# The last transform stage of a convolution, done once for all 640 channels

## The chip, the cores and the metric

The kernel runs on one core of one Trainium2 chip. The metric is device time in microseconds, the median of three runs. TensorE is called PE, its weight loads PEld, VectorE DVE, ScalarE ACT, GpSimd POOL, and SyncE, whose queue issues nearly all DMAs, SP.

## What is computed

Cut to what matters (S = 2048 rows, D = 640 channels, F = 1728):

```python
xn  = layernorm(x)                                   # x is A_q
ks  = sum_t  k_pad[:, t:t+S, :] * shift_k[:, 3 - t]  # four taps along the rows
kv  = ks * v
y   = irfft(rfft(kv, 4096) * rfft(ssm_k, 4096))[:, :S] + kv * ssm_D   # causal convolution per channel
A   = xn * y
B   = (sigmoid(xn @ w_gate) * (xn @ w_up)) @ w_down
out = x + A + B
```

## The kernel before

Two things share the core: the gated products B on PE, with their evictions, and the convolution A, whose four transform stages are small matmuls on PE with elementwise work between them.

**B.** The 2048 rows go in four blocks `tr` of 512. A block's normalized rows are transposed to `xnT`; then for each of 14 chunks `fc` of 128 hidden columns `rec_fc` (L761) makes a gate and an up product, five matmuls of 512 columns each (L773), and `rec_evac` makes `hT` from a sigmoid on ACT and a product on DVE (L727 to L740). `rec_down` (L780) then does the block's down product in pieces of seven matmuls of 320 columns (L789), added to `acc` by DVE (L800). `acc` holds x at first and the output in the end.

**A.** The 640 channels go in two halves, each in five groups of 64 channels; `idx` 0 to 9 counts the groups (`NI` = 10, `NSUB` = 5). A group's way:
- `rec_kv` (L451): ten DVE operations of 1024 elements for the taps (L469 to L474) and the product with v (L487) give `kvt`. The channel order inside a group is two runs of eight.
- `rec_st1` (L489): twice 32 matmuls on tiles of 32 rows (L507), of the filter (`ht`) and of `kvt`, evicted to `T`.
- `rec_st2` (L516): four times 32 matmuls (L527), evicted to `S`.
- `rec_prod` (L541): the complex product on DVE; from group 3 on a DMA swaps the halves of the partitions (`P<-S`, L547).
- `rec_st3` (L569): twice 8 matmuls of 128 columns (L579), evicted to `V`, a tile with all of one half: 64 × 2 × 80 columns.
- `rec_st4` (L595) per half, once its five groups are through: four units `u`, each in two parts of 64 matmuls on tiles of 32 × 32 (L611). A matmul has 80 columns, the channels of one quarter `g` of the half. Each unit reloads a piece of the normalized rows from memory (`xnd`, 512 pieces of 640 bytes), evicts twice 640 elements, and does two DVE operations of 1280 elements (L619, L620): times xn, plus `acc`.

`V` has one buffer, which first holds the early weights `wv` (gate and up, chunks 0 to 7, used by blocks 0 and 1), then the first half's V, then the second's. So the second half's first eviction to V waits for the first half's last stage. The reloads of the first half go to the two `xq` buffers (which hold normalized rows before), those of the second to the buffers of k and v. The PSUM tags are `c` (three slots of two banks) and `g` (two slots of one).

**Order.** Nothing is scheduled when it is built: every operation is recorded by `_Plan.op` (L152) with what it reads and writes, and `ORDER` (L80) lists in which order all 979 are issued; `ON_DVE` (L124) names those evictions that DVE does in ACT's place. `_Plan.emit` (L193) gives out buffers in that order. Each engine and the SP queue take their own operations in this order. In ORDER the first half's eight parts of L611 stand between stage 2 of group 6 and stage 3 of group 5, and the second half's between the last stage 3 and the down products of block 3. The last two row tiles' down products (`PRM["ML"]` = 14) also wait for the convolution's add (`cv`).

Of the kernel before, what the change touches and what calls it, by code (L numbers as in the profile page):

```python
# [18 lines left out]
S = 2048  # L19
# [16 lines left out]
NI = 2 * NSUB  # L36

# [5 lines left out]
def _dft_tables():  # L43
# [37 lines left out]
    1, 42, 5, 0, 6, 8, 7, 71, 72, 10, 12, 13, 11, 14, 73, 74, 75, 91, 86, 16, 87, 607, 76, 608, 4, 96, 77, 78, 97, 79,  # L81
    104, 88, 18, 60, 81, 82, 83, 625, 80, 92, 98, 643, 84, 85, 93, 99, 645, 89, 90, 63, 644, 94, 626, 43, 148, 100,
    62, 15, 66, 2, 149, 101, 102, 64, 150, 61, 68, 103, 621, 609, 623, 154, 611, 610, 622, 612, 624, 153, 67, 157,
    617, 619, 17, 65, 613, 158, 151, 59, 618, 615, 152, 650, 58, 620, 57, 651, 652, 56, 44, 29, 30, 627, 628, 629,
    630, 19, 31, 45, 32, 631, 633, 614, 616, 108, 20, 106, 632, 634, 639, 640, 641, 105, 39, 22, 155, 3, 642, 646, 24,
    599, 107, 156, 648, 647, 601, 600, 21, 26, 649, 635, 121, 109, 113, 602, 111, 603, 637, 27, 119, 604, 605, 112,
    606, 25, 636, 117, 638, 118, 663, 664, 666, 673, 110, 115, 116, 679, 122, 120, 123, 23, 125, 114, 674, 35, 37,
    677, 680, 133, 683, 681, 36, 653, 654, 682, 136, 684, 127, 661, 38, 162, 135, 657, 658, 134, 137, 662, 33, 675,
    665, 659, 660, 34, 130, 164, 47, 95, 676, 678, 667, 51, 128, 172, 163, 655, 656, 831, 165, 668, 671, 669, 49, 53,
    131, 739, 124, 166, 48, 50, 741, 28, 670, 832, 54, 126, 740, 167, 168, 833, 672, 742, 181, 183, 52, 689, 129, 691,  # L90
    721, 41, 171, 159, 723, 690, 692, 722, 132, 724, 298, 182, 160, 40, 694, 693, 696, 169, 161, 302, 730, 731, 732,
    733, 695, 697, 178, 716, 179, 180, 718, 743, 170, 173, 175, 195, 174, 300, 744, 745, 698, 717, 138, 197, 196, 176,
    177, 303, 201, 199, 700, 299, 185, 699, 198, 184, 187, 719, 720, 200, 685, 192, 301, 701, 186, 189, 702, 202, 686,
    687, 688, 188, 218, 203, 205, 707, 193, 204, 69, 46, 190, 194, 139, 709, 703, 708, 143, 217, 227, 207, 705, 141,
    55, 704, 710, 228, 229, 230, 706, 711, 191, 233, 140, 231, 725, 142, 305, 232, 812, 727, 712, 714, 213, 214, 726,
    206, 728, 713, 216, 219, 715, 734, 220, 772, 234, 221, 215, 209, 736, 210, 208, 222, 735, 737, 771, 224, 304, 746,
    70, 761, 226, 211, 729, 223, 212, 738, 749, 225, 252, 253, 762, 235, 764, 249, 251, 255, 263, 264, 236, 238, 254,
    750, 759, 752, 250, 265, 266, 269, 240, 267, 268, 747, 760, 237, 270, 256, 239, 748, 763, 288, 243, 290, 786, 751,
    257, 291, 244, 289, 788, 241, 260, 765, 242, 753, 271, 258, 261, 247, 766, 144, 245, 769, 272, 248, 262, 273, 754,
    757, 767, 285, 246, 287, 318, 407, 259, 768, 319, 275, 286, 294, 755, 296, 320, 410, 321, 274, 770, 324, 276, 322,  # L100
    277, 295, 787, 789, 325, 307, 278, 323, 292, 756, 758, 293, 834, 279, 280, 790, 281, 308, 836, 835, 837, 315, 326,
    309, 310, 282, 327, 782, 317, 297, 838, 811, 413, 283, 316, 306, 784, 312, 839, 311, 313, 783, 284, 785, 340, 341,
    354, 342, 355, 777, 840, 773, 329, 358, 867, 360, 146, 328, 356, 331, 409, 779, 775, 357, 359, 314, 330, 361, 774,
    778, 776, 780, 822, 351, 334, 335, 332, 791, 333, 362, 823, 343, 824, 363, 825, 344, 345, 412, 352, 145, 813, 353,
    815, 411, 336, 814, 147, 337, 338, 826, 346, 348, 404, 339, 816, 347, 383, 781, 408, 364, 366, 368, 369, 427, 817,
    828, 406, 365, 428, 827, 431, 376, 429, 405, 414, 433, 349, 829, 819, 430, 367, 818, 370, 371, 432, 792, 830, 820,
    372, 797, 434, 799, 373, 435, 866, 374, 793, 821, 350, 795, 436, 375, 806, 415, 418, 424, 425, 426, 794, 384, 796,
    416, 417, 463, 808, 419, 421, 464, 385, 386, 798, 387, 800, 388, 807, 377, 437, 389, 809, 465, 802, 466, 378, 810,
    801, 420, 804, 454, 439, 390, 379, 380, 803, 805, 449, 451, 438, 422, 450, 440, 467, 841, 842, 856, 843, 391, 443,
    468, 444, 469, 392, 423, 857, 846, 453, 859, 848, 393, 394, 460, 395, 470, 396, 397, 860, 9, 849, 861, 452, 455,  # L110
    886, 852, 864, 461, 457, 456, 441, 442, 881, 883, 462, 862, 398, 471, 399, 472, 401, 863, 400, 445, 926, 458, 446,
    490, 928, 489, 850, 447, 448, 459, 865, 851, 499, 500, 868, 870, 473, 505, 853, 488, 501, 502, 503, 854, 474, 476,
    475, 844, 506, 485, 479, 855, 487, 480, 845, 491, 477, 478, 847, 483, 504, 507, 858, 486, 484, 493, 481, 869, 508,
    482, 496, 492, 871, 498, 877, 497, 571, 494, 495, 578, 882, 521, 527, 509, 884, 510, 511, 512, 879, 522, 872, 878,
    887, 880, 523, 528, 533, 534, 513, 874, 529, 530, 531, 873, 875, 532, 514, 892, 515, 516, 524, 885, 893, 535, 894,
    536, 381, 907, 901, 585, 517, 876, 592, 525, 895, 519, 902, 526, 518, 549, 903, 402, 904, 896, 897, 905, 899, 888,
    906, 927, 537, 539, 898, 550, 890, 541, 538, 540, 542, 520, 553, 543, 554, 551, 555, 552, 929, 900, 545, 889, 544,
    556, 931, 891, 403, 557, 546, 558, 908, 910, 930, 932, 909, 547, 921, 911, 559, 923, 560, 917, 561, 919, 562, 922,
    918, 548, 924, 565, 566, 569, 563, 564, 570, 912, 920, 567, 913, 568, 572, 914, 915, 382, 573, 925, 933, 575, 934,
    938, 935, 916, 579, 580, 582, 574, 576, 581, 583, 584, 577, 963, 944, 965, 945, 586, 947, 939, 941, 587, 588, 589,  # L120
    936, 590, 591, 593, 594, 942, 596, 595, 970, 964, 597, 598, 937, 940, 943, 946, 973, 974, 967, 948, 950, 972, 949,
    966, 968, 952, 951, 969, 958, 953, 975, 954, 959, 962, 978, 955, 971, 960, 976, 956, 957, 961, 977
]
ON_DVE = [  # L124
    101, 103, 45, 133, 654, 136, 134, 34, 139, 426, 525, 895, 915, 575, 582, 589, 595
# [3 lines left out]
class _Op:  # L129
    __slots__ = ("engs", "alloc", "seq", "deps", "touch", "size", "on", "pri", "nb", "slack", "start", "end", "turn", "ni")  # L130


class _Plan:
# [18 lines left out]
    def op(self, engs, r=(), w=(), c=(), alloc=(), pri=0.0, size=0.0, nb=0.0, slack=0.0, ni=0):  # L152
        o = _Op()
        o.engs, o.pri, o.size, o.nb, o.slack, o.ni = engs, pri, size, nb, slack, ni
# [31 lines left out]
    def table(self):  # L186
        dve = set(ON_DVE)
        for i in ORDER:
            o = self.ops[i]
            o.on = next(iter(o.engs)) if len(o.engs) == 1 else "DVE" if i in dve else "ACT"  # L190
        return [self.ops[i] for i in ORDER]
# [27 lines left out]
def kernel(  # L219
# [23 lines left out]
    srow = A_shift_k.rearrange("(h g d) m -> g h (d m)", h=2, g=G)  # L243
    drow = A_ssm_D.rearrange("(h g d) -> g h d", h=2, g=G)
# [12 lines left out]
    ident = cst.tile([P, P], BF16, name="ident")  # L257
    acc = cst.tile([P, NQ, DM], BF16, name="acc")
    wd = cst.tile([P, NFC, DM], BF16, name="wd")
    Ft = cst.tile([P, 2 * K1 + 2 * P], U16, name="Ft")  # L260
    Mt = cst.tile([P, K1, 3 * K2], U16, name="Mt")
    At = cst.tile([P, 3, 2 * N2], U16, name="At")
    Bt = cst.tile([P, N2, 2, N1], U16, name="Bt")
    Fb = Ft.bitcast(F16)
# [7 lines left out]
    jk = cst.tile([P, DM], BF16, name="jk")  # L272
# [4 lines left out]

    SLOTS = {"w": 4, "xq": 2, "xnT": 1, "sig": 2, "bs": 1, "kt": 1, "vt": 1, "ht0": 1, "ht1": 1, "kvt": 2,
             "ta": 1, "tb": 1, "T": 2, "S": 2, "P2": 1, "V": 1, "c": 3, "g": 2}
    SHAPE = {  # L280
        "w": ([P, NC, 512], BF16), "xq": ([P, 4, DM], BF16), "xnT": ([P, NC, 512], BF16), "sig": ([P, 512], BF16),
        "bs": ([P, 12], F32), "kt": ([P, N2 + 3, HALF], BF16), "vt": ([P, N2, HALF], BF16),
        "ht0": ([P, 16, 2, N2], BF16), "ht1": ([P, 24, 2, N2], BF16), "kvt": ([P, 2, N2, JS], BF16),
        "ta": ([P, N2, 2, JS], BF16), "tb": ([P, N2, 2, JS], BF16), "T": ([P, 2 * K1, 2, JS, G], BF16), "S": ([P, 2, 2, JS, G * K1], BF16),
        "P2": ([P, 2, JS, G * K1], BF16), "V": ([P, N2, 2, HALF], BF16),
# [5 lines left out]
    def make(b, tag, i):  # L291
        shape, dt = SHAPE[tag]
        if b.startswith("pst"):
            shape, dt = [P, NC, P], BF16
        if b == "wv":
            shape, dt = [P, 4, NC, 512], BF16
        if b in ("xk", "xv"):
            shape, dt = [P, 2, 2, 4 * DM // 2], BF16
        pool = ps if tag in ("c", "g") else wk
        return pool.tile(shape, dt, name=f"{tag}{i}", tag=f"{tag}{i}")  # L300
# [149 lines left out]
    def by_j(t):  # L450
        return t.rearrange("p b n j -> p (b n j)").rearrange("p (j b n) -> p j b n", j=JS, b=2)  # L451
# [479 lines left out]
```

## Time and profile before

| what | value |
|---|---|
| median of 3 runs | 254.18 us (254.09, 254.18, 258.87) |
| span of the profiled execution (no other time of it is given) | 252.8 us |
| PE, DVE, ACT busy | 239.6, 202.2, 177.2 us |
| last stage, L611 on PE | 1024 matmuls, in two stretches: 152.6 to 169 and 223.7 to 236.4 us |
| first stage 1 of kv on PE | 67.98 us |
| last stage 3 on PE starts | 221.87 us |
| last matmul ends, last DVE operation ends | 247.5, 247.9 us |

The page of the profile gives busy times by engine and by slice; a group row gives line, engine, operation, output and inputs, shapes and count, then busy us and mean ns of one, then the engine's idle time just before them and what ended it. A matmul's own duration is mostly latency that overlaps the next one's, so its cost is read from the spacing, which the chain of work gives. Busy time on PE includes the end of the last matmul's latency.

### The profile page before, as it was taken

To read this page: it belongs to the slowest core of one execution; us is meant where nothing else is said; L and a number is where in the kernel's file an instruction comes from. 1 tells how busy PE (TensorE), PEld (TensorE's weight loads), DVE (VectorE), ACT (ScalarE), POOL (GpSimd) and SP (SyncE) were. 2 spreads that over 40 slices of the span, in tenths; PEclk is the share of its full clock that TensorE was granted. 3 is DMA by queue.
4 is the path that set the end of the run, shared out by engine and by line. 5 is a ranking of instruction groups with operands and counts; after the bars stand their busy time and mean duration, and the time that the engine had idled before them with its cause. 6 is when DMAs were issued, how large, how long until landed. Compare 5 with 4: busy or idle time off the path is not lost.

```text
span 252.8 us, 9452 instructions
## 1 busy us (share of the span) xinstructions
PE 239.6 (95%) x4211; PEld 145.6 (58%) x4245; DVE 202.2 (80%) x339; ACT 177.2 (70%) x260; POOL 0.7 (0%) x6
## 2 busy tenths in 40 slices
PE   7899999999999999999999999999999999999891
PEld 2754446764454557676554646677765554466571
DVE  4622635787999999999999999999999986878821
ACT  3723699686799997677998997867789886451100
POOL 1000000000000000000000000000000000000000
PEclk9999999999999999999999999999999999999998
DMA  6999999999993189699998995535617597001762
GB/s 173 336 299 241 278 214 159 174 132 211 226 144 104 65 245 233 141 148 127 175 195 227 244 226 141 91 75 167 130 29 175 135 275 191 3 3 31 158 174 62
DMA packets 90976, 41.44 MB, mean 164 GB/s; under 512 B 66736, under 2 KB 88056, under 8 KB 90616
## 3 DMA queue, kind: packets, MB, share of 16 engines
q1 hardware_dynamic: 90744, 40.52, 74.5%
q8 instruction: 33, 0.54, 1.0%
q10 hardware_dynamic: 192, 0.33, 0.4%
q14 instruction: 7, 0.06, 0.1%
HBM read 30.61 MB, written 5.24 MB: 142 GB/s over the span
## 4 chain that ended last, share of the span: by engine, by line
PE 66%; DVE 14%; DMA 7%; ACT 5%; issue 3%; ACTq 1%; SPq 0%; DVEq 0%
PE g L773 29%; PE g L789 20%; PE c L527 5%; PE c L611 3%; DMA P<-S 3%; PE c L579 3%; DMA w<-in_B_w_up_dram 2%; PE c L507 2%; ACT S L313 2%; DVE ta L474 2%; PE c L753 2%; DMA acc<-in_A_q_dram 1%; ACT sig L738 1%; DVE kvt L487 1%; DVE hT L740 1%
## 5 line engine op out<-in xcount | busy, mean ns | idle before, releaser
L773 PE MATMUL g<-xnT,w 128*128 128x512 bf16 x355 | 89.1, 379 | 2.4 <-DVE hT L740 0.5
L789 PE MATMUL g<-wd,hT 128*128 128x320 bf16 (+1 forms) x462 | 66.3, 295 | 0.2
L773 PEld LDWEIGHTS <-w 128*128 128x128 bf16 x380 | 35.0, 98 | 38.6 <-issue 1.3
L789 PEld LDWEIGHTS <-hT 128*128 128x128 bf16 x462 | 42.9, 98 | 16.8 <-issue 0.7
L313 ACT CAST S<-c 128x1024 bf16<-128x1024 f32 x40 | 40.0, 1031 | 2.8 <-PE c L527 2.3
L740 DVE TENSOR_TENSOR hT<-sig,g 128x512 bf16<-128x512 bf16 x32 | 21.9, 686 | 18.8 <-PE g L773 18.2
L773 PE MATMUL g<-xnT,V 128*128 128x512 bf16 x131 | 32.6, 379 | 0.6 <-DVE hT L740 0.2
L738 ACT ACTIVATE sig<-g 128x512 bf16<-128x512 f32 x32 | 19.5, 610 | 11.9 <-PE g L773 11.9
L313 ACT CAST V<-c 128x1024 bf16<-128x1024 f32 x20 | 20.4, 1026 | 4.8 <-PE c L579 3.7
L800 DVE TENSOR_TENSOR acc<-g,acc 128x320 bf16<-128x320 f32 (+1 forms) x33 | 15.6, 477 | 9.6 <-PE g L789 9.3
L527 PEld LDWEIGHTS <-Mt 64*128 64x128 f16 x1280 | 20.0, 95 | 5.5 <-issue 5.0
L316 ACT ACTIVATE T<-c 128x1024 bf16<-128x1024 f32 x20 | 20.2, 1032 | 3.7 <-PE c L507 3.6
L527 PE MATMUL c<-T,Mt 64*128 64x64 bf16 x1280 | 22.5, 190 | 0.2
L487 DVE TENSOR_TENSOR kvt<-ta,vt 128x1024 bf16<-128x1024 bf16 x10 | 21.5, 2146 | 0.1
L773 PEld LDWEIGHTS <-V 128*128 128x128 bf16 x140 | 13.0, 97 | 14.7 <-issue 0.8
L313 ACT CAST T<-c 128x1024 bf16<-128x1024 f32 x18 | 17.9, 1021 | 1.7 <-PE c L507 1.7
L732 ACT ACTIVATE sig<-g 128x512 bf16<-128x512 f32 x18 | 11.0, 610 | 7.6 <-PE g L773 5.9
L474 DVE TENSOR_TENSOR ta<-ta,tb 128x1024 bf16<-128x1024 bf16 x20 | 13.8, 689 | 0.4
L469 DVE TENSOR_TENSOR tb<-kt,sT 128x1024 bf16<-128x1024 bf16 x20 | 13.7, 683 | 0.1
L560 DVE TENSOR_TENSOR S<-S 128x1024 bf16<-128x1024 bf16 x20 | 13.5, 684 | 0.1
L579 PE MATMUL c<-At,S 128*128 128x128 f16 x160 | 12.8, 219 | 0.8 <-DVE S L566 0.7
L579 PEld LDWEIGHTS <-S 128*128 128x128 bf16 x160 | 10.8, 98 | 4.5 <-DVE S L566 2.1
(84 smaller groups left out, 243.6 us busy)
## 6 DMA issues: line engine op xcount, KB each, us to landing
w<-in_B_w_gate_dram SPq DMA_DIRECT2D x7, 640.0 KB, 6.4
w<-in_B_w_up_dram SPq DMA_DIRECT2D x7, 640.0 KB, 6.4
P<-S SPq DMA_DIRECT2D x14, 256.0 KB, 3.9
kt<-in_A_k_dram SPq DMA_DIRECT2D x8, 320.0 KB, 7.2
vt<-in_A_v_dram SPq DMA_DIRECT2D x8, 320.0 KB, 6.3
xnd<-xq SPq DMA_DIRECT2D x4, 640.0 KB, 5.1
ht<-in_A_ssm_k_dram SPq DMA_DIRECT2D x16, 96.0 KB, 4.6
wd<-in_B_w_down_dram SPq DMA_DIRECT2D x3, 480.0 KB, 10.2
```

The costliest lines, as they stand in the source:

```text
L313: fa = lambda: nc.scalar.copy(out=out_fn(), in_=in_fn())
L316: fa = lambda: nc.scalar.activation(out_fn(), in_fn(), ACT.Copy, scale=scale)
L469: dve(1024, 2, lambda: nc.vector.tensor_tensor(tl[c][:], sl(tl[kb], 3 - m), sh(m), ALU.mult) if c != o else nc.vector.tensor_tensor(tl[c]. ...
L474: dve(1024, 2, lambda: nc.vector.tensor_tensor(tl[a][:], tl[a][:], tl[c][:] if c != o else tl[c].rearrange("p b n j -> p n b j"), ALU.add) ...
L487: dve(1024, 1 if kt else 2, lambda: nc.vector.tensor_tensor(by_j(tl[o]) if kt else tl[o][:], tl[a].rearrange(form), sl(tl[vb], 0).rearrang ...
L527: nc.tensor.matmul(tl[c][:, b, 64 * kk:64 * kk + 64], lhsT=Mb[rows, k, 64 - 64 * r:192 - 64 * r], rhs=tl[T][rows, 2 * k + r].rearrange("p ...
L579: nc.tensor.matmul(o, lhsT=tl[S_][:, b, 0, j, :], rhs=Ab[:, 2 if zc else 0, :], start=True, stop=zc)
L738: act(512, lambda: nc.scalar.activation(tl[sg][:], pv(0), ACT.Sigmoid), r=[pk(0)], w=[(sg,)], alloc=[(sg, "sig")], pri=pri - 2000)
L740: dve(512, 1, lambda: nc.vector.tensor_tensor(hT[:, fc, :], tl[sg][:], pv(1), ALU.mult), r=[pk(1), (sg,)], w=[(hk, fc)], pri=pri - 2000)
L773: nc.tensor.matmul(tl[c][:], lhsT=w()[:, k, o:o + P], rhs=tl[X][:, k, :], start=(k == 0), stop=(k == NC - 1))
L789: nc.tensor.matmul(tl[pd[i]][:, 0:d1 - d0], lhsT=hT[:, fc, t4 * P:(t4 + 1) * P], rhs=wd[:, fc, d0:d1], start=(fc == 0), stop=(fc == NFC - 1))
L800: dve(d1 - d0, 1, lambda i=i, m=m, pd=pd, d0=d0, d1=d1: nc.vector.tensor_tensor(acc[:, m, d0:d1], tl[pd[i]][:, 0:d1 - d0], acc[:, m, d0:d1 ...
```

## The change

The last stage is done once, after all ten groups, for all 640 channels. `VV` is one tile of 21 chunks of 1024 columns; a group's V is two chunks, `Vc[:, idx]`. It shares memory with early buffers: chunks 0 to 9 with `wv`, chunks 10 to 15 with the two `xq` buffers, the scratch `jk`, the identity and the tables `FE`, chunks 16 to 20 with `ht`. `over` makes the first write of the second half's V wait for the users of `jk`, `ident` and `FE`, and groups 8 and 9 for those of `ht`. The quarter `g` now counts over all channels (`g * 160 + half * 80`), and a group's 16 channels of a quarter are one run, not two runs of eight; the filter is loaded with 16 DMAs in place of 32. A unit of `rec_st4` is 64 matmuls of 160 columns, whose moving operand is ten pieces of 16 columns; there are eight units. All reloads go to the buffers of k and v, in 256 pieces of 1280 bytes. The down products of the last two row tiles no longer wait for `cv`; the stores do. ORDER (956 operations) and ON_DVE are new.

```diff
-    ident = cst.tile([P, P], BF16, name="ident")
-    Ft = cst.tile([P, 2 * K1 + 2 * P], U16, name="Ft")
-    jk = cst.tile([P, DM], BF16, name="jk")
+    Ft = cst.tile([P, 2 * K1], U16, name="Ft")
+    VV = cst.tile([P, 2 * NI + 1, NCH], BF16, name="VV")
+    V5 = VV.rearrange("p c n -> p (c n)")[:, 2 * NSUB * NCH:2 * NSUB * NCH + 6 * NCH]
+    jk = V5[:, 4 * DM * 2:4 * DM * 2 + DM]
+    ident = V5[:, 9 * DM:9 * DM + P]
+    Vc = VV[:, 0:2 * NI].rearrange("p (s h) n -> p s (h n)", h=2).rearrange("p s (n r d) -> p s n r d", n=N2, r=2)
...
     def load_h(half, part, pri, nb=0.0):
         for g in range(G):
-            for p in range(2):
-                c0 = (half * G + g) * HALF + p * JH
-                dma(lambda e, g=g, p=p, c0=c0: e.dma_start(tl[b][g * N1:(g + 1) * N1, :, p, :], h3[:, c0 + j0:c0 + j1, :]), 32 * (j1 - j0), 128,
+            c0 = g * CG + half * HALF + CJ * s0
+            dma(lambda e, g=g, c0=c0: e.dma_start(tl[b][g * N1:(g + 1) * N1, :, :], h3[:, c0:c0 + n, :]), 32 * n, 128,
...
     def rec_st3(idx, pri):
-            ev(1024, lambda co=co: tl[V].rearrange("p n r d -> p (n r) d")[:, :, co:co + JS],
+            ev(1024, lambda b=b: Vc[:, idx].rearrange("p n r d -> p (n r) d")[:, :, b:CJ:2],
...
-    def rec_st4(half, pri, out):
-        for u in range(4):
-            for ih in range(2):
-                def f(u=u, cs=cs, ih=ih):
-                    for i in (2 * ih, 2 * ih + 1):
-                        for r in range(2):
-                            for g in range(G):
-                                for q in range(4):
-                                    n2 = 16 * q + 4 * u + i
-                                    nc.tensor.matmul(tl[cs[g // 2]][32 * q:32 * q + 32, g % 2, 80 * i:80 * i + 80],
-                                                     lhsT=Bb[32 * g:32 * g + 32, n2, r, :], rhs=tl[V][32 * g:32 * g + 32, n2, r, :],
+    def rec_st4(pri):
+        for v in range(8):
+            def f(v=v, cs=cs):
+                for i in range(2):
+                    for r in range(2):
+                        for g in range(G):
+                            for q in range(4):
+                                n2 = 16 * q + 2 * v + i
+                                nc.tensor.matmul(tl[cs[g // 2]][32 * q:32 * q + 32, g % 2, CG * i:CG * i + CG],
+                                                 lhsT=Bb[32 * g:32 * g + 32, n2, r, :], rhs=Vc[32 * g:32 * g + 32, :, n2, r, :],
...
-                if s == NSUB - 1:
-                    rec_st4(0, ct(s + PRM["ST4"]), False)
-        rec_st4(1, ct(NI - 0.2), False)
+        rec_st4(ct(NI - 0.2))
```

## The prediction

> **What bounds the kernel now.** I read the busy shares first, then the stages, then the group of the line that changes, then what waits. The page gives the span, 252.8 us, and for the profiled execution no other time; the median of the three runs is 254.18 us, so 1.38 us lie outside the span, and I add them at the end.
>
> ```profile
> span 252.8 us, 9452 instructions
> PE 239.6 (95%) x4211; PEld 145.6 (58%) x4245; DVE 202.2 (80%) x339; ACT 177.2 (70%) x260; POOL 0.7 (0%) x6
> PE   7899999999999999999999999999999999999891
> DVE  4622635787999999999999999999999986878821
> PEclk9999999999999999999999999999999999999998
> ```
>
> TensorE is busy in all but the first and last slices, at full clock. VectorE is idle at the start and full from slice 11 to 32. So two engines may be the bound in the middle. The stages (columns: length, busy us of PE, PEld, DVE, ACT, POOL, clock, DMA) say how nearly full each is:
>
> ```profile
> 63.00:205.00 142.00, 139.12 (x2923) 85.64 (x2947) 136.50 (x203) 120.42 (x153) 0.00 (x0) 1.00 0.76 159
> 205.00:222.30 17.30, 16.48 (x187) 8.84 (x188) 14.11 (x22) 11.26 (x15) 0.00 (x0) 1.00 0.47 131
> 222.30:248.00 25.70, 23.57 (x651) 16.43 (x649) 16.41 (x27) 4.87 (x7) 0.00 (x0) 1.00 0.40 95
> ```
>
> From 63 to 222.3 us (the convolution, with the gate and up products of blocks 1 to 3 between) DVE idles 5.5 + 3.2 = 8.7 us and PE 2.9 + 0.8 = 3.7 us. ACT has 27.6 us free. After 222.3 us (last stage of the second half, last down products) DVE idles 9.3 us and ACT 20.8: there PE alone is the bound.
>
> ```profile
> L611 PE MATMUL c<-V,Bt 32*32 32x80 bf16 x1024 | 10.8, 203 | 1.4 <-issue 1.3
> L611 PEld LDWEIGHTS <-Bt 32*32 32x32 f16 x1024 | 8.7, 87 | 5.4 <-issue 5.0
> L507 PE MATMUL c<-Ft,ht 32*128 32x64 f16 x320 | 4.2, 189 | 0.0
> L620 DVE TENSOR_TENSOR acc<-acc,xq 128x1280 bf16<-128x1280 bf16 x4 | 3.3, 819 | 0.0
> L314 DVE CAST T<-c 128x1024 bf16<-128x1024 f32 x2 | 2.4, 1218 | 0.0
> L313 ACT CAST V<-c 128x1024 bf16<-128x1024 f32 x20 | 20.4, 1026 | 4.8 <-PE c L579 3.7 <-PE c L581 0.8
> ```
>
> The last stage is 1024 matmuls of 80 columns. Their 203 ns each are latency that overlaps; the pace is in the chain of work that ended last:
>
> ```profile
> 121.75 0.34 PE c L507 x32
> ...
> 152.71 0.62 PE c L611 x64
> ```
>
> **The change, part by part.**
>
> *Half the matmuls (rec_st4).* 64 matmuls take 0.62 us, 9.7 ns each, so 16 units are 9.9 us. The built program has 512 of 160 columns in 8 units. 64-column matmuls of L507 go at 0.34/32 = 10.6 ns: fewer columns are no faster, so the pace is that of weight load and matmul pairs and not of columns. I keep 0.62 us a unit: 8 units, 5.0 us, **−5.0 us of PE work**. Bounds: −5.0, and 0 if the pace goes with the columns (1.24 us a unit). The nearest row on columns is L507's, so I take −5.0.
>
> The order of the program says where these 5.0 us go. After the last stage-3 matmul there are 8 units in both kernels (before: 8 of the second half), with 16 down pieces and two gate/up pieces. All that is removed is removed between 63 and 222 us: the 8 units of the first half at 152 to 168 us.
>
> A rule that speaks against this: the Trainium skill, "TensorE: Matmul & The Clock Gate", section "The mechanism" (of row/col tiling), says that a weight load overlaps matmuls in flight only when their row group differs. Here three of four successive pairs have the same row group, so by that rule a pair would wait for its predecessor's columns, by an estimate with its 2.4 GHz 33 ns now and 67 ns after, and 8 units would cost as much as 16: the sum would be that of rival C below. The 9.7 ns above disagree with it at 80 columns. No run here shows it at 160.
>
> *Burst starts.* 13 bursts of L611 wait 5.0 us for issue on the weight queue, of which PE itself shows 1.3 us; the rest lies under the end of the matmuls before. After, 8 bursts remain. I take −0.5; bounds −1.9 (5 of 13) and 0.
>
> *DVE in the convolution.* From first kv-fed stage 1 to last stage 3 the plans differ on DVE by: 7 last-stage multiplies and adds out (7 × 0.82 = −5.7), 2 evictions of S and 2 of V moved here from ACT (4 × 1.22 = +4.9), a halo copy, a norm and the gate work (+0.40 + 0.44 + 0.42). Sum **+0.4 us**: DVE gets nothing back. ACT loses 8 × 0.69 + 5 × 1.03 and some small ones, about −10 us, but it had slack. So PE is relieved by 5.0 us, DVE stays, and the stage can shrink only by what DVE now idles, 8.7 us. Part of that is the conv's own latency (of the DMA swap P<-S 4.71 us at 211.5 in the chain, covered by no DVE work) and not PE's doing. Bounds: −5.5 (all PE's gain with the burst starts) and 0. I take half of PE's 5.0: **−2.5 us**, the burst starts in it.
>
> *kv multiplies, new channel order.* Same elements, same strides of the long operands (32 and 160 bytes); inner pieces of 16 instead of two of 8. L487 took 2146 ns, L469 683. Nothing: bounds ±0.06 us for each of 80 (the spread of L469, L470 and L474 is 9 ns); I take 0.
>
> *Evictions into V with a step of two elements.* Evictions to T write pieces of two and take 1.02 us, those to V pieces of eight 1.03. So 0.
>
> *SP.* 16 DMAs of ht less (32 to 16, each twice as large), one more for the tables, 8 reloads of xn as before. SP issues less by some 8 us (16 × 0.5), but PE shows only 1.1 us of DMA waits after 63 us. 0; bounds −1.0 and +1.0, since the shift row, FE and part of ht now stand ahead of weights: the shift matmul is PE's fourth group instead of its twentieth, and must find them landed by 10.3 us. The first weights had landed by 9.0 and FE is 64 KB behind them, where a slice moved 336 GB/s: in time. The last of the four early weight blocks has 3.0 MB up to its end, 0.44 more than before; the first two slices moved 3.2 MB by 12.6 us, and it is first read at about 15.8: covered.
>
> *Added waits.* VB's first eviction, on ACT, waits for the stores of all xn, for jk, ident and FE; behind it in ACT's queue are S and gate evictions. The last store of xn is issued 129 places of the order before it, with 12 gate or up products of 1.08 us and 10 down pieces of 0.95 on PE between; a store takes 5.1 us. Covered. V's first eviction waits for the last gate product that reads the early weights, now 53 places before it (12 before). In return the second half's V no longer waits for the first half's last stage.
>
> *The tail.* PE's work from last stage 3 on is the same: 2 × 1.08 + 8 × 0.62 + 15.2 for down = 22.3 us in a stretch of 25.0 us (222.5 to 247.5). DVE's grows from 17.0 to 21.0 us (one V eviction, four operations of 0.82, less 0.4), ACT's last-stage evictions from 4 to 15 (10.4 us). Both still fit under 25.0 us, DVE with 4 us to spare. The stores of rows 0 to 7 must wait for four units' adds, some 12 us after the last stage 3 instead of 10, and three last stores stand behind the last unit's add: +0.5; bounds −1.0 (bursts) and +3.0.
>
> Sum: −2.5 + 0.5 = −2.0; the start 0. Span 250.8, plus 1.38: **252.2 us**. With the bounds: −5.5 − 1.0 − 1.0 = −7.5 (246.7) to 0 + 1.0 + 3.0 = +4.0 (258.2).
>
> **Rivals.**
>
> *A: all of PE's gain comes through.* DVE's idle time is there because PE is late, and closes. −5.5 + 0 = 248.7 us. For it: PE is 98% busy from 63 to 205 us. Against: so is DVE, at 96%, with more work after.
>
> *B: nothing comes through.* DVE sets the middle, and the longer tail shows: 0 + 0.5, 254.7 us. For it: DVE's sum rises.
>
> *C: slower, the wide matmul takes twice as long.* L579's 8 matmuls of 128 columns take 0.45 us on the whole array, 0.44 ns a column; 80 columns are 35 ns, and at 9.7 ns apart 3.6 matmuls are in flight. If that is a limit, 160 columns go at 19.4 ns, a unit is 1.24 us, and all 8 lie in PE's tail: +5.0, while the middle still gives −2.5: 254.2 − 2.0 + 5.0 = 257.2 us. It decides from a unit of 0.62 + 2.0/8 = 0.87 us on, 13.6 ns a matmul. For it: each moving operand also becomes ten pieces of 16 columns, 4 KB apart, and no row has such an operand. Against: L507 has 64 × 0.44/10.6 = 2.7 in flight without being faster, so the count in flight sets no pace there, and the output stays in one piece. The Trainium skill, "Advanced Engine Details and Errata", section "Memory Cachelines", says that subsequent accesses should stay in a 16-byte line of SBUF; 16 columns are two full lines. By that rule the pieces would cost nothing; no run here shows it.
>
> *D: slower, the tail's DVE lags.* 21.0 us of DVE work with waits for ACT, reloads and PSUM buffers may not close in 25 us. If a reload of xn (4.0 us to landing now) is found late twice, +5.0 − 2.5: 256.7 us. It decides when the waits exceed DVE's 4 us of slack by 2.5.
>
> That the change does not do what it says is excluded: the built order has 512 of the wide matmuls and no half-wise last stage.
>
> **How the numbers follow.** Forecast 0.42, A 0.25, B 0.14, C 0.09, D 0.10. Two per cent, about what a measurement of this kernel can tell from no change, is 5.1 us: faster is below 249.1, slower above 259.3. A lies at the lower edge, 0.17 of it below; the forecast's own range (249.5 to 254.5, the halves of its bounds) lies within, its lowest 0.03 below. Faster: 0.20. Slower: 0.03 of C, 0.03 of D, and 0.06 of the forecast and B for stalls of a wholly new order that counts can't see: 0.12. Same: 0.68. I predict 252.2 us; 8 times in 10 it lies between 247.0 and 257.5, the bounds of the sum, with a part of A, C and D beyond them left out.
>
> **What would show it.** Right: 512 matmuls with 64 in about 0.62 us; PE busy lower by about 5 us; DVE at 97% or more between 63 us and the last stage 3, which ends about 2.5 us earlier; a tail of 25 to 26 us. Wrong: a unit over 0.87 us (C); DVE idle in the tail while waiting for xk, xv (D); DVE's idle time in the middle below 4 us with PE following (A); a stall of PE before 60 us, where the sum has none.

## The result, and the profile after

The changed kernel takes 256.62 us (median of 13 runs, 254.79 to 260.78) beside 254.52 us for the kernel before: ratio 1.0077, 95% interval 1.005 to 1.0105, so 2 us slower. The prediction was 252.2 us. Here and below a time is the median of all executions, while the ratio leaves out those over 1.5% above the fastest of their kernel, so where the two disagree (experiments 6, 12 and 13) the ratio counts. The profiled execution of the changed kernel took 258.3 us with a span of 256.5; in it TensorE's clock halved for 3.4 us near the end, and that is 1.6 us of it.

The page of the kernel after:

```profile
span 256.5 us, 8447 instructions
PE 238.2 (93%) x3733; PEld 141.8 (55%) x3733; DVE 204.5 (80%) x340; ACT 181.0 (71%) x259; POOL 0.7 (0%) x6
PE   7999999999999999899999999979999999699790
DVE  4514533799999999999999999999999993979640
PEclk9999999999999999999999999999999999999977
```

PE lost 1.4 us of busy time, not 5 (3.0 without the 1.6 that the clock added). Its row has three new holes: a 7 in slice 27 (167 to 173 us), a 6 in slice 35 (218 to 224, just ahead of the last stage 3) and a 7 in slice 38 (237 to 244, in the last stage). The clock falls in the last two slices. For the account I cut both kernels at the same events: from the first kv-fed stage 1 to the end of the last stage 3, and from there to the last matmul. Kernel before (columns: length, busy us of PE, PEld, DVE, ACT, POOL, clock, DMA):

```profile
67.98:222.48 154.50, 150.95 (x3088) 92.60 (x3115) 146.19 (x218) 127.92 (x162) 0.00 (x0) 1.00 0.71 152
222.48:247.51 25.03, 23.39 (x648) 16.37 (x647) 15.94 (x25) 4.87 (x7) 0.00 (x0) 1.00 0.40 95
```

Kernel after:

```profile
67.04:222.93 155.89, 147.93 (x2609) 88.86 (x2609) 146.20 (x216) 123.83 (x151) 0.00 (x0) 1.00 0.67 146
222.93:250.70 27.77, 25.81 (x649) 16.84 (x646) 19.61 (x29) 12.05 (x18) 0.00 (x0) 0.94 0.45 131
```

In the middle PE is busy 3.0 us less and DVE exactly as long as it was, yet the stretch is 1.4 us longer, because it starts 0.9 us earlier and its end has not moved forward: the last stage 3 starts at 222.32 us (221.87 before). PE's idle time went from 3.55 to 7.96 us. The true difference is larger: the trace of before has 346 weight loads of gate and up products in this stretch and only 319 matmuls, and the missing records leave some 25 gaps of about 0.05 us, 1.35 us in all. By an estimate, then, PE had 4.4 us less to do and idled 2.2 us before. The tail grew by 2.7 us, 1.6 of them the clock. The rows of the operations that changed:

```profile
L332 ACT CAST VV<-c 128x1024 bf16<-128x1024 f32 x17 | 22.2, 1323 | 3.3 <-PE c L594 2.3 <-DMA P<-S 0.9
L623 PE MATMUL c<-VV,Bt 32*32 32x160 bf16 x512 | 6.4, 234 | 2.0 <-issue 2.0
L623 PEld LDWEIGHTS <-Bt 32*32 32x32 f16 x512 | 4.4, 87 | 5.0 <-issue 4.1 <-DVE hT L746 0.4
L333 DVE CAST VV<-c 128x1024 bf16<-128x1024 f32 x3 | 3.9, 1302 | 0.3 <-PE c L594 0.3
```

The eviction with a step of two takes 1323 ns on ACT where the plain one took 1026. The pace of the wide matmuls is in PE's timeline of the tail (start, length, operation, then idle time before it):

```profile
235.01 0.76 PE L623 MATMUL c<-VV,Bt 32*32 32x160 bf16 x64
235.70 2.07 PE L800 MATMUL g<-wd,hT 128*128 128x320 bf16 x14
237.70 0.76 PE L623 MATMUL c<-VV,Bt 32*32 32x160 bf16 x64
238.39 2.08 PE L800 MATMUL g<-wd,hT 128*128 128x320 bf16 x14
240.40 0.74 PE L623 MATMUL c<-VV,Bt 32*32 32x160 bf16 x62
242.94 0.24 PE L623 MATMUL c<-VV,Bt 32*32 32x160 bf16 x2 [1.79 <-issue]
243.11 7.59 PE L800 MATMUL g<-wd,hT 128*128 128x320 bf16 x56
```

From 235.01 to 235.70 a unit takes 0.69 us (0.62 before, 232.67 to 233.29). In the last unit PE stops for 1.79 us before its last two matmuls, waiting for nothing that the profile shows ("issue"). I take such stops for waits for instructions; the last section says why. The 56 down matmuls behind it take 7.59 us; in most other runs here they take 5.97.

What PE waits for from 130 to 224 us, kernel after (us in total, times, longest):

```profile
PE c L594 <- DVE S L580: 2.0, 1, 2.0
PE c L541 <- issue: 1.6, 1, 1.6
PE c L521 <- DVE kvt L503: 0.5, 1, 0.5
PE g L800 <- DVE acc L811: 0.5, 1, 0.5
PE g L784 <- DVE hT L751: 0.5, 1, 0.5
PE c L541 <- ACT VV L332: 0.5, 1, 0.5
```

and before:

```profile
PE c L579 <- DVE S L566: 0.7, 2, 0.5
PE g L773 <- DVE hT L740: 0.5, 1, 0.5
PE g L773 <- issue: 0.2, 1, 0.2
```

So the freed time is there, as waits: one of 2.0 us just ahead of the last two stages 3, one of 1.6 us for issue, and pieces of half a microsecond. The experiments ask why.

### The profile page after: what moved, and what is told of

Read it like the earlier page. It is cut to its first block, busy times and chain, and to the rows that moved or that the text cites. A ratio compares the mean times of both kernels' runs of the same rounds, so it can differ in the third digit from the quotient of the medians.

```text
span 256.5 us, 8447 instructions
## 1 busy us (share of the span) xinstructions
PE 238.2 (93%) x3733; PEld 141.8 (55%) x3733; DVE 204.5 (80%) x340; ACT 181.0 (71%) x259; POOL 0.7 (0%) x6
## 4 chain that ended last, share of the span: by engine, by line
PE 44%; DVE 23%; ACT 15%; DMA 6%; SPq 5%; issue 4%; ACTq 0%; DVEq 0%
PE g L784 25%; PE g L800 11%; DMA P<-S 4%; DVE S L574 3%; DVE S L580 3%; DVE S L578 3%; ACT VV L332 3%; PE c L541 3%; ACT S L332 3%; DMA acc<-in_A_q_dram 3%; PE c L623 2%; ACT VV L666 2%; DVE P L565 2%; ACT VV L660 2%; SPq L396 2%
## 5 line engine op out<-in xcount | busy, mean ns | idle before, releaser
L800 PE MATMUL g<-wd,hT 128*128 128x320 bf16 (+1 forms) x462 | 68.7, 300 | 1.8 <-DVE acc L811 1.4
L332 ACT CAST S<-c 128x1024 bf16<-128x1024 f32 x38 | 37.5, 1025 | 5.0 <-PE c L541 5.0
L784 PE MATMUL g<-xnT,VV 128*128 128x512 bf16 x140 | 32.6, 379 | 0.1
L332 ACT CAST VV<-c 128x1024 bf16<-128x1024 f32 x17 | 22.2, 1323 | 3.3 <-PE c L594 2.3
L811 DVE TENSOR_TENSOR acc<-g,acc 128x320 bf16<-128x320 f32 (+1 forms) x33 | 15.6, 477 | 11.1 <-PE g L800 10.8
L335 ACT ACTIVATE T<-c 128x1024 bf16<-128x1024 f32 x19 | 18.9, 1028 | 4.3 <-PE c L521 4.3
L784 PEld LDWEIGHTS <-VV 128*128 128x128 bf16 x140 | 13.0, 98 | 14.7
L332 ACT CAST T<-c 128x1024 bf16<-128x1024 f32 x19 | 19.0, 1017 | 1.5 <-PE c L521 1.4
L594 PEld LDWEIGHTS <-S 128*128 128x128 bf16 x160 | 10.8, 98 | 6.0 <-DVE S L580 3.8
L574 DVE TENSOR_TENSOR S<-S 128x1024 bf16<-128x1024 bf16 x20 | 13.5, 688 | 0.3
```

The costliest lines, as they stand in the source:

```text
L332: fa = lambda: nc.scalar.copy(out=out_fn(), in_=in_fn())
L335: fa = lambda: nc.scalar.activation(out_fn(), in_fn(), ACT.Copy, scale=scale)
L574: dve(n, 2, lambda b=b: nc.vector.tensor_tensor(X(b), X(b), H(b), ALU.mult), r=[(Z, b, 0)] + sr, w=[(S_, "p", b)], pri=pri + 0.01)
L594: nc.tensor.matmul(o, lhsT=tl[S_][:, b, 0, j, :], rhs=Ab[:, 2 if zc else 0, :], start=True, stop=zc)
L784: nc.tensor.matmul(tl[c][:], lhsT=w()[:, k, o:o + P], rhs=tl[X][:, k, :], start=(k == 0), stop=(k == NC - 1))
L800: nc.tensor.matmul(tl[pd[i]][:, 0:d1 - d0], lhsT=hT[:, fc, t4 * P:(t4 + 1) * P], rhs=wd[:, fc, d0:d1], start=(fc == 0), stop=(fc == NFC - 1))
```

## The experiments

Theories for the middle: PE's sum sets it (*P*); DVE's sum sets it (*D*, rival B); the two bind in turn, so that both must be relieved (*J*); the dearer evictions ate the gain (*step*); the last group's own chain sets the end (*K*); or the written order does, in which engines wait for one another at fixed places, so that work taken from one becomes its idle time (*O*). Each ratio is to the kernel before, run beside it. In every one the landmark is the start of the last stage 3 in the one execution that was profiled. Experiments 14 to 16 change nothing ahead of it, and still show it 0.4 to 0.85 us earlier than the kernel they change; so a shift of less than 0.9 us says little, and the ratio decides.

**1. The evictions' step.** After, with V written in one run (the channels come out in another order):

```diff
-            ev(1024, lambda b=b: Vc[:, idx].rearrange("p n r d -> p (n r) d")[:, :, b:CJ:2],
+            ev(1024, lambda b=b: Vc[:, idx].rearrange("p n r d -> p (n r) d")[:, :, JS * b:JS * b + JS],
```

> The changed kernel, but stage 3 is evicted into V in runs of eight columns instead of with a step of two (as before the change). Nothing else moves; the channels of y inside each run of 16 come out in another order, so a part of the result is permuted. V evictions took 1323 ns on ACT with the step against 1026 before the change, 17 of them on ACT. Theory 'step': the step costs the difference and much of it lies on the path: V evictions back to about 1030 ns, ACT busy 5 us less, time 256.6 - 1.5 to 2.5 = 254.1 to 255.1 us. Theory 'DVE sets the middle': the evictions get cheaper but ACT had slack; only the two on DVE in the middle count: 256.1 to 256.6 us.

Measured: 257.50 us, ratio 1.0133 (1.0097 to 1.0168). The evictions fall to 1018 ns on ACT and 1220 on DVE, ACT's busy time by 4.4 us, the landmark by 0.7 us to 221.59, within the spread; the time does not fall. *Step* is not the cause.

**2. Evictions from DVE to ACT.** After, with seven of the 18 evictions in ON_DVE given back:

```diff
-    31, 90, 96, 126, 127, 129, 132, 133, 207, 286, 328, 454, 475, 489, 511, 525, 537, 635
+    31, 90, 96, 126, 127, 129, 132, 133, 525, 537, 635
```

> The changed kernel with seven evictions that its list gave to DVE handed back to ACT: two of S and two of V in the middle, and three of the others (two of T, one halo). The computation is the same. DVE loses 4 x 1.2 + 2 x 1.2 + 0.4 = 7.6 us between 67 and 222 us, ACT gains 7 us. Theory 'DVE sets the middle': the last stage 3 comes 3 to 5 us earlier, 252 to 254 us. Rival 'ACT is late where DVE was not': ACT's queue is strict and its eviction of V costs 1.3 us, time 256 us or more. Theory 'PE sets the middle': 256.6 us, no change.

Measured: 258.45 us, ratio 1.0162 (1.0128 to 1.0196). DVE 197.7 us busy instead of 204.5, ACT 186.8; landmark 224.22. Against *D*, though ACT's new work muddles it.

**3 and 4. One engine relieved, kernel before.** Half of the first half's last stage left out (256 matmuls, the sums incomplete):

```diff
-                        for r in range(2):
+                        for r in range(2 if half else 1):
...
```

> The kernel before, with only one of the two accumulating matmuls in the first half's last stage: 256 of its 512 matmuls are left out (so y of the first half is incomplete), all evictions, loads and DVE work stay. PE loses 2.5 us between 152 and 169 us and nothing else changes: this is the change's saving on PE by itself, at half its size. Theory 'PE sets the middle': 254.5 - 2.5 = 252.0 us. Theory 'DVE sets the middle': 254.0 to 254.5 us.

Measured: 253.42 us, ratio 0.9981 (0.9963 to 0.9999); landmark 221.11: 0.5 of 2.5 us came through (0.03 to 0.9 by the interval). And the first half's eight multiplies and adds (L619, L620) left out:

```diff
-            dve(1280, 2, lambda X=X: nc.vector.tensor_tensor(X(0), X(0), X(1), ALU.mult), r=yk, ...
+            dve(1280, 2, lambda X=X: nc.vector.tensor_tensor(X(0), X(0), X(1), ALU.mult) if half else None, r=yk, ...
...
```

> The kernel before, without the first half's eight multiply and add operations of the last stage on DVE (y of the first half is not added). PE, ACT and the DMAs keep their work; DVE loses 8 x 0.82 = 6.6 us, 5.7 of it before the last stage 3. Theory 'DVE sets the middle': the last stage 3 comes 3 to 5.5 us earlier, 249 to 251.5 us. Theory 'PE sets the middle': 254 to 254.5 us.

Measured: 254.37 us, ratio 1.0007 (0.9987 to 1.0027); landmark 221.65. Neither *P* nor *D* alone.

**5. All of it gone, kernel before.** Matmuls, evictions, multiplies and adds of the first half's last stage left out:

```diff
+                f = f if half else lambda: None
                 pe(630, 64, f, r=vr_ + [("B",), (xb, u)] + ([(cs[0], "a")] if ih else []), ...
-                   ..., r=[(cs[e],)], w=[yk[e]], pri=pri)
+                   ..., r=[(cs[e],)], w=[yk[e]], pri=pri, skip=not half)
```

> The kernel before without the whole last stage of the first half (its 512 matmuls, 8 evictions, 4 products and 4 sums; the loads stay): 5.0 us less on TensorE, 6.6 us less on VectorE and some 5 us less on ScalarE, all in the middle. Earlier runs took 2.5 us from TensorE alone (gain 0.6) and 6.6 us from VectorE alone (gain 0). Theory J, the two engines bind in turn, so that a gain needs both relieved: last stage 3 starts at 216 to 218 us instead of 221.9, time 248 to 250. Theory O, the written issue order and its hand-offs set the landmarks and no engine's sum does: last stage 3 not before 220.5, time 252.5 to 254. It is also the most that moving this stage out of the middle could ever give.

Measured: 253.86 us, ratio 0.9963 (0.994 to 0.9987); landmark 221.19. This is the most that moving the stage out of the middle could give in the order as written: 0.9 us, 1.5 at the far end of the interval. Its middle, cut half a microsecond behind the landmark:

```profile
67.98:221.70 153.72, 146.39 (x2579) 88.11 (x2603) 140.98 (x212) 122.95 (x154) 0.00 (x0) 1.00 0.69 151
```

PE idles 7.3 us (some 1.3 of them missing records, as in before), DVE 12.7, ACT 30.8, and the end stands where it stood. No engine's sum sets it, nor the two together: *P*, *D* and *J* fall for this kernel.

**6 and 7. DVE relieved on the conv's own operations.** Nine of the third sums of the short convolution left out (6.2 us), in after and in before:

```diff
-            dve(1024, 2, lambda: nc.vector.tensor_tensor(tl[a][:], tl[a][:], tl[c][:], ALU.add),
+            dve(1024, 2, lambda: None if c == t2 and idx else nc.vector.tensor_tensor(tl[a][:], tl[a][:], tl[c][:], ALU.add),
```

> The kernel after without the last of the three sums of the short convolution in every piece but the first (9 x 0.69 = 6.2 us less on VectorE, all between 67 and 222 us, on the engine only and not on ScalarE). TensorE is already 5 us lighter there. Theory J or rival B (VectorE binds once TensorE is lighter): last stage 3 at 218 to 219.5 instead of 222.3, time 3 to 5 us under the kernel after (251.5 to 253.5). Theory O: last stage 3 within 0.7 us of 222.3, time 256 to 257.

> The same nine sums left out of the kernel before (6.2 us less on VectorE; TensorE keeps its 5 us). Theory J: TensorE still binds, gain under 1 us, time 253 to 254. If the sums count because they stand in the chain of the convolution (unlike the products and sums left out of the earlier run, which stand outside it): gain 3 to 5 us, as in the kernel after. Theory O: no gain.

Measured: after 256.78 us, ratio 1.0088 (1.0056 to 1.012), landmark 222.00; before 254.08 us, ratio 0.9991 (0.9967 to 1.0015), landmark 221.32. *D* falls where it should have been strongest. The landmark of after is the clock's in part: the granted clock was 0.51 from 220.6 to 224.1 us, and the five gate matmuls ahead of the last stage 3 took 1.75 us instead of 1.07; without that it would stand near 221.3 (an estimate).

**8 and 9. The last group's exchange.** Group 9 with four half products on DVE instead of two transfers and two products:

```diff
-               SWAP=(3, 4, 5, 6, 7, 8, 9), ...
+               SWAP=(3, 4, 5, 6, 7, 8), ...
```

> The kernel after with the half exchange of the last piece (idx 9) computed by four half products on VectorE instead of two transfers and two whole products: the 5.1 us of the transfers in the chain that ends in the last stage 3 go, VectorE gets 1.4 us more. Nothing is left out. Theory K (the end of the middle is set by the last piece's chain: evictions of S, exchange, ten products, stage 3, each in its written place): the last stage 3 starts 1.5 to 3 us earlier, at 219.3 to 220.8 instead of 222.3, and the time falls by 1 to 2.5 us to 254 to 255.6. If TensorE's or VectorE's sum sets it: no gain, or up to 1.4 us slower (256.6 to 258).

> The same edit in the kernel before. TensorE's idle time before the last two stages 3 is 0.5 us there (2.0 in the kernel after), so theory K expects a gain of at most 0.5 to 1 us: last stage 3 at 221 to 221.9, time 253.4 to 254.4. If VectorE's sum sets the middle: up to 1.4 us slower, 255 to 256.

Measured: after 256.42 us, ratio 1.0084 (1.0057 to 1.0111), landmark 222.71; before 254.19 us, ratio 0.9998 (0.998 to 1.0016), landmark 221.45. *K* as I had put it missed: 5 us of transfers are gone from the chain, and its end is where it was. The timeline of this kernel says why:

```profile
211.54 1.27 DVE L751 TENSOR_TENSOR hT<-sig,g 128x512 bf16<-128x512 bf16 x2
212.27 2.32 PE L784 MATMUL g<-xnT,w 128*128 128x512 bf16 x10 [0.49 <-DVE hT L751]
...
214.70 0.69 DVE L751 TENSOR_TENSOR hT<-sig,g 128x512 bf16<-128x512 bf16 x1 [1.88 <-PE g L784]
...
215.42 2.11 DVE L571 TENSOR_TENSOR P<-S 64x1024 bf16<-64x1024 bf16 x3
...
221.17 0.62 PE L594 MATMUL c<-At,S 128*128 128x128 f16 x8 [1.37 <-DVE S L580]
```

PE waits 0.49 us for DVE to free a PSUM buffer; then DVE waits 1.88 us for PE to fill it, because the next gate product (888 in ORDER) stands ahead of the half products (L571), whose input was ready; then PE waits 1.37 us for what came late by that. No work is missing anywhere; it stands in the wrong place.

**10. The place alone.** The kernel of 8 with the four half products put ahead of 888 (514 to 517; one of them stood behind a product of L574 as well):

```diff
-    868, 883, 909, 509, 477, 885, 886, 887, 504, 898, 502, 888, 505, 514, 515, 517, 519, 900, 889, 891, 516, 899, 522,
+    868, 883, 909, 509, 477, 514, 515, 517, 516, 885, 886, 887, 504, 898, 502, 888, 505, 519, 900, 889, 891, 899, 522,
```

> The kernel after without the last piece's exchange transfers (as in the run before this) and with the four half products moved in the written order from behind to ahead of one product of the feed-forward part (pieces 514 to 517 ahead of 888); no work is added or removed against that run. Theory O (the engines wait for each other at written places): the 1.88 us for which VectorE waited there is used, TensorE's wait of 1.4 to 2.0 us before the last two stages 3 goes, the last stage 3 starts at 220 to 221 instead of 222.3 to 222.7, and the time falls by 1 to 2 us to 254.6 to 255.6. If an amount of work or a transfer sets the landmark: it stays at 222 to 222.7 and the time at 256.4.

Measured: 254.40 us, ratio 1.0017 (0.999 to 1.0043), against 1.0084 (1.0057 to 1.0111) for the same work in the old places; landmark 220.76.

```profile
210.86 1.27 DVE L751 TENSOR_TENSOR hT<-sig,g 128x512 bf16<-128x512 bf16 x2
211.85 2.33 PE L784 MATMUL g<-xnT,w 128*128 128x512 bf16 x10 [0.80 <-DMA w<-in_B_w_gate_dram]
212.16 2.83 DVE L571 TENSOR_TENSOR P<-S 64x1024 bf16<-64x1024 bf16 x4
...
219.23 0.61 PE L594 MATMUL c<-At,S 128*128 128x128 f16 x8
```

DVE goes straight on at 212.16, and stage 3 finds its input: no wait at 219.23. Four instructions moved by a few places brought 2 us on the landmark, and 1.7 us of time by the two ratios, whose intervals do not meet; leaving out 6.2 us of DVE's work had brought 0.3 on the landmark (about 1.0 without the clock) and no time. Theory *O* stands for this place. In after itself the exchange stands there too: DVE waits 1.88 us for PE at 213.73, then 2.15 us for the transfer. Only taking away both gave the 2 us; 8 took away the transfer alone and gained nothing.

**11 to 13. What sets the middle then?** With contiguous evictions as in 1; with five more moves of one or two places, at PE's waits of 0.34 to 0.61 us; and without the nine sums as in 6:

> The same with V evicted in one run instead of with a step of two (the channels within each run of 16 come out permuted; 20 evictions of 1.02 to 1.22 us instead of 1.30 to 1.32). Theory O, the small waits for V's eviction (0.22 and 0.49 us) go too, and with the wait at the end used up they now come through: another 0.3 to 1 us, 254 to 255. If the eviction's cost is off the path, as the earlier run of it alone showed: the same as the run beside it within 0.4 us.

> The kernel of the run with the four half products moved, with five more moves of one or two places in the written order (229 behind 740, 813 ahead of 314, 761 behind 275, 823 ahead of 400, 705 and 706 ahead and behind 715), each at a wait of TensorE of 0.34 to 0.61 us at 96, 103, 122, 130 and 167 us; together 2.4 us of waits. No work is changed. If the written places still set the middle: last stage 3 1 to 2 us earlier than 220.8, time 252.4 to 253.6. If VectorE's sum sets it now: TensorE's waits only move, last stage 3 within 0.4 us of 220.8, time 254 to 254.8.

> The kernel of the run with the four half products moved, without nine of the sums of the short convolution (6.2 us less on VectorE, as in the earlier run in the unchanged order, which gained nothing). If VectorE's sum sets the middle once the place at its end is mended (rival B): last stage 3 at 216 to 218.5, time 250.5 to 252.5. If other written places hold it: last stage 3 at 219.5 to 220.8, time 253.4 to 254.4.

The five moves in ORDER:

```diff
-    715, 705, 242, 246, 200, 706, ...
+    705, 715, 706, 242, 246, 200, ...
-    229, 723, 138, 253, 734, 62, 256, 257, 254, 740, ...
+    723, 138, 253, 734, 62, 256, 257, 254, 740, 229, ...
-    314, 813, ...
+    813, 314, ...
-    761, 275, ...
+    275, 761, ...
-    400, 823, ...
+    823, 400, ...
```

Measured: 254.94 us, ratio 1.0031 (1.0004 to 1.0059), landmark 220.23; 255.43 us, ratio 1.0037 (0.9996 to 1.0077), landmark 222.71; 255.18 us, ratio 1.0008 (0.9967 to 1.0049), landmark 220.81. None gains clear of the noise: rival B's 250.5 to 252.5 us for 13 is ruled out, and *O*'s forecasts for 11 and 12 missed as well. The five moves took out three of their five waits and most of a fourth, and made another: PE waits 1.18 us for DVE at 110 us (0.47 without them). The landmark of 12 is not theirs alone: the granted clock was 0.51 from 171.3 to 174.8 us, and 14 down matmuls took 3.75 us there instead of 2.08 in 10; without these 1.67 us it would stand near 221.0 (an estimate). A gain of up to 1 us over 10 is not excluded by the intervals of 12 and 13. What holds the end at 220.8 us is not settled.

**14 to 16. The tail.** Half of the last stage's matmuls left out of after (one of its two matrices):

```diff
-                    for r in range(2):
+                    for r in range(1):
...
```

> The kernel after with only half of the last stage's products (one of the two matrices: 256 matmuls less, 8 units of 0.35 us instead of 0.69, 2.7 us less on TensorE, all behind the last stage 3). If the tail is TensorE's and its instruction stream's: last stage 3 stays at 222, the time falls by 2.5 to 3.5 us to 253 to 254. If the tail is set by VectorE's and ScalarE's work on the pieces: under 1 us faster, 255.7 to 256.6.

Measured: 253.84 us, ratio 0.9978 (0.9958 to 0.9999); landmark 221.93. Against 1.0077 that is 2.5 us. The trace shows more than 2.7 us of matmuls gone: a unit takes about 0.3 us instead of 0.69 (3.1 us in eight), the 1.95 us of waits for issue in the last stage are not there, and PE waits 1.57 us for DVE's additions (L811) in their place. So the tail is PE's, though with some 3 us less on PE the additions begin to hold it up; how much of the gain the matmuls alone brought, this run does not separate. And both kernels without the stores of row tiles 0 to 13 of 16:

```diff
-            dma(lambda e, q=q: e.dma_start(oq4[q]...
+            dma(lambda e, q=q: None if m0 < 14 else e.dma_start(oq4[q]...
```

> The kernel after without the stores of the first 14 of 16 rows (12 transfers, 2.3 MB; their output is not written). If the output's traffic is what stalls TensorE's instructions near 241 us and stretches the last stage: the stall of 1.5 to 1.8 us in the last unit is gone, the 64 matmuls stay at 0.69 us, and the time falls by 1.5 to 2.5 us to 254 to 255. If the stall has nothing to do with the stores: it stays, and the time stays within 0.7 us of 256.6.

> The kernel before without the stores of the first 14 rows (their output is not written), beside the same edit in the kernel after, which gained 1.1 us and lost the stall in the last stage. If the stores disturb both tails alike: 1 to 1.5 us faster, 253 to 253.5, and the two instruction waits of 0.53 and 0.76 us in the last stage are gone. If it is the new tail that collides with them: under 0.4 us faster, 254.1 to 254.5.

Measured: after 255.55 us, ratio 1.0038 (1.0011 to 1.0066), 1.0 us less than with stores; before 252.29 us, ratio 0.9938 (0.9914 to 0.9961), 1.6 us less. So stores cost both tails. But they cost at different places. In after the stop in the last unit is gone in the profiled execution, the fastest of its twelve:

```profile
239.49 0.86 PE L623 MATMUL c<-VV,Bt 32*32 32x160 bf16 x64
240.28 5.97 PE L800 MATMUL g<-wd,hT 128*128 128x320 bf16 x56
```

In before the two waits for issue stay (0.50 and 0.48 us), and most of the gain lies behind the last matmul: 3.9 us to the end of the span instead of 5.3.

No version here that does the whole work beats the kernel before; the one of 10 equals it.

## Why the prediction was wrong

First the account. Where a run's own time is known, 1.8 us lie outside its span (253.92 − 252.1 in experiment 5, 258.3 − 256.5 after); the prediction's 1.38 set one execution's span against another's time, so the profiled execution before took about 254.6 us. After, without the 1.62 us of the clock, took 256.7. Of these 2.1 us, 0.45 are the later last stage 3; the time from there to the last matmul grew from 25.64 to 28.38 − 1.62 = 26.76 (+1.1); the rest of the span behind the last matmul from 5.3 to 5.8 us (+0.5). These are two executions: the 0.45 is within the spread of the landmark, and the stop in the last unit, 1.79 us here, is 0.42 to 2.07 in other kernels with the same tail.

- *Half the matmuls, −5.0, a unit kept at 0.62 us*: the count was right, the unit takes 0.69 (10.8 ns a matmul, not 9.7). 8 × 0.07 = 0.56 us, all in the tail, where experiment 14 shows that PE's time counts.
- *The rule on weight loads* ("TensorE: Matmul & The Clock Gate", "The mechanism", of the Trainium skill) would have put a pair of 160 columns at 67 ns by the estimate in the prediction. The trace disagrees with it here as at 80 columns: 10.8 ns. That *the pieces of 16 columns cost nothing*, which the prediction drew from "Advanced Engine Details and Errata", "Memory Cachelines", of the Trainium skill, agrees with the trace to within the 1.1 ns a matmul by which width and pieces together slowed it.
- *DVE in the middle, +0.4*: right, 146.19 and 146.20 us.
- *The middle, −2.5, "half of PE's 5.0"*: **this step failed**. It was +0.45. Of the 5.4 us of L611 taken out, 1.3 were filled with six more gate and up matmuls (346 weight loads in the stretch before, 352 after, 0.22 us each), as the stretch starts 0.9 us earlier. The other 4, and 1.4 us more, became waits. I had asked which engine's sum bounds the stretch and split the difference; experiments 3 to 7 show that no sum does, 5 above all: with the whole stage left out, 0.9 us comes through, and 2.5 lies beyond the interval. 10 shows that the place of four DVE instructions was worth 2 us. What holds the rest of the freed time stays open. The prediction read the new ORDER for what work it moves and not for who waits for whom in it. A reading beside it was wrong too: the exchange of 4.71 us at 211.5 was not "covered by no DVE work", DVE did 2.80 us in that time.
- *Rival A* fell with that. *Rival B* had the middle right, "nothing comes through", by a mechanism that did not hold: "DVE sets the middle" is refuted by 4, 6 and 13. Its time, 254.7, fell short mostly by what the tail grew.
- *Burst starts, −0.5*: wrong in sign. PE's waits for issue at the last stage went from L611's 1.3 us to L623's 2.0.
- *Evictions with a step of two, 0*: wrong in size, +0.30 us on ACT (17 of them, 5.0 us) and +0.08 on DVE, and right in effect: experiments 1 and 11 gain nothing by mending it. I had costed the step by a row with pieces of two elements, not with a step between single ones.
- *SP and the start, 0*: right to 0.9 us; the first kv-fed stage 1 comes at 67.04 us instead of 67.98.
- *The tail, +0.5*: the sign was right, its size +1.1 to the last matmul and +0.5 behind it. The 1.1 are 0.56 of the wide unit, and 1.95 us of waits for issue instead of 1.29; the sum had PE's tail unchanged. The early stores that the prediction named do not make the 0.5: without them (15) 5.8 us still lie behind the last matmul. The last stores, which it named too, may; no run here leaves them out.
- *Rival C* (257.2) and *Rival D* (256.7) came nearest to 256.62, by luck. C decided from 0.87 us a unit on; 0.69 is below. For D, DVE's 19.6 us fit in the tail (it had 15.9 before, not 17.0), and PE waited for nothing of it beyond small pieces.
- *A sum*: half of the upper bound gives 255.2 for the forecast's own range, not 254.5. No chance hangs on it.

Two things remain open: why the end of the middle stays at 220.2 to 222.7 us in all sixteen runs but one (experiment 2), most of them with one engine relieved; and when the granted clock halves behind a wait and when it does not.

## What to carry to other kernels

Where engines run orders written out in advance and hand each other buffers, the time between two landmarks need not be the larger of the engines' sums, and here it was not; before crediting freed time, follow the engine past the freed place to the next instruction that waits for another engine, and ask whether that one comes earlier too. Work added on the engine that bounds a stretch (here TensorE in the tail) shows in the time, while the stretch that work was taken from may give nothing back. When a relief of some microseconds moves nothing, look for two engines that wait in turn within a few microseconds, and move the one instruction that stands between.

## What the runs showed of the hardware

- TensorE stops in bursts of short matmuls, waiting for nothing that the profile shows. That it waits for instructions is inferred. The instruction queue in the page of the profile, before and after:

```profile
q8 instruction: 33, 0.54, 1.0%
```

```profile
q8 instruction: 29, 0.48, 0.8%
```

  0.54 MB in 33 packets is 16.4 KB each. 512 matmuls with their 512 weight loads less make 4 packets less; 256 of each less make 2 (31 packets in experiment 3, 27 in 14). So a packet holds 256 instructions, by an estimate from these four. The stop in the last unit comes before its last two matmuls in all nine kernels here with this tail and its stores (0.42 to 2.07 us), as at a packet's edge. That the packet waits behind the stores fits the run without them, which has no stop; it is not shown directly.
- In four of the eighteen profiled executions the granted clock halved for about 3.4 us while PE had work: from 243.5 us in after (0.51 in the mean over 243.4 to 246.9; the 56 down matmuls there took 7.59 us instead of 5.97), 240.8 in 11 (7.64), 220.7 in 6 (after) and 171.3 in 12. Each time PE had ended a wait of 1.52 to 2.20 us less than 0.9 us earlier. Waits of 1.79 us (8) and 2.07 us (13) were not followed by it.
- ACT's eviction of 1024 elements from PSUM with an output step of two 2-byte elements takes 1323 ns, contiguous runs of eight 1018 to 1026; on DVE 1302 and 1220.
